# Summing phi(K) of four tiles on GpSimd ahead of the matmuls, with new instruction lists, in a two-layer linear-attention and MLP kernel

## The chip, the cores and the metric

The kernel runs on one core of a Trainium2 chip. The metric is the device time of one execution in microseconds (us); less is better. TensorE (PE) multiplies matrices, VectorE (DVE), ScalarE (ACT) and GpSimd (POOL) work on tiles of 128 partitions, and SyncE (SP) issues transfers. Each engine runs its own list of instructions in order; semaphores order them between engines.

## The reference

Input x has 2048 rows of 512 features in bfloat16. Two layers follow each other with the same weights, each an attention block and an MLP with a residual:

```python
def _A_ref(x, wqkv, wo):                       # 32 heads of 16
    q, k, v = heads_of(x @ wqkv)
    phi = lambda t: jnp.where(t > 0, t + 1, jnp.exp(t)) + 1e-6
    pq, pk = phi(q), phi(k)
    kv = jnp.einsum("bhsd,bhse->bhde", pk, v)
    z = jnp.einsum("bhsd->bhd", pk)            # column sums of phi(K)
    num = jnp.einsum("bhqd,bhde->bhqe", pq, kv)
    den = jnp.einsum("bhqd,bhd->bhq", pq, z)[..., None] + 1e-6
    return rows_of(num / den) @ wo

def _B_ref(x, w1, b1, w2, b2):
    y = _layernorm(x)
    return gelu(y @ w1 + b1) @ w2 + b2

x = x + _A_ref(_layernorm(x), A_wqkv, A_wo)
x = x + _B_ref(_layernorm(x), w1, b1, w2, b2)  # 512 -> 1792 -> 512
```

Both lines come twice. `heads_of` and `rows_of` stand for reshapes.

The change concerns `z`, the sum of phi(K) over all 2048 rows, in the first layer.

## The kernel before

The 2048 rows are four chunks (`c`) of four tiles (`k`) of 128 rows; a tile's number is `st = 4c + k`. The first layer takes the chunks in the order `C0=(3, 0, 1, 2)`, so its first four tiles are 12 to 15. For each tile the kernel normalises the rows, transposes them (four tiles on TensorE, twelve by DMA), multiplies by the K columns of wqkv, forms phi(K), and adds phi(K) against the normalised rows into four PSUM banks (`G`). Q is made by chunk. The products of the first layer are then turned into one matrix per head block (`KV`, `M`), and the MLP follows.

Names of operations, as the lists have them (`0` is the layer, then the chunk or tile):

- `warm`: dummy matmuls on a constant at the start, `N_WARM` of 512 columns and `N_WARM2` of 128 (L699).
- `stats`, `aggr`, `veps`, `pow`, `nmr`, `norm`, `cen`, `ysc`: the steps of a norm (L743, L745, L756, L758, L775, L778 on ScalarE or L783 on VectorE, L724, L768). `pow` is on GpSimd, and so is `nmr`.
- `PTA` and `TA`: the transposes on TensorE (L806) and by DMA on SP's queue (L793).
- `K0_st` (L861), `Q0_c_k` (L892, by tile L879), `G0_st` (L962): groups of four matmuls.
- `exp`, `relu`, `min`, `phi`: the steps of phi (L831, L842, then L844 and L848, or L835 and L837 where `phi` is taken as a maximum straight from PSUM). `phi` of a few tiles is on GpSimd (L848).
- `Z0_c`: the column sums of one chunk's phi(K): 16 matmuls with a single column of ones as the moving operand, phi(K) as the stationary one, four for each of four output columns (L943). `zs0_c` adds the result to `zs` on VectorE (L949, L952).
- `ZH`: the same sums taken from a running total. `za` adds a tile's phi(K) into the float32 tile `zacc` (L915, on GpSimd if not named otherwise), `zhi` and `zlo` split the total into two bfloat16 parts (L921, L924), `ZH` sums these with 8 matmuls (L931, L932), and `zsh` copies the result to `zs` (L935).
- `D0` (L1086), `ln`, `rec` (L1088, L1090), `pr` (L1094): the denominators of chunks 0 and 1 and the products with them, `pr` partly on GpSimd.
- `KV` (L1017), `M` (L1040), `WO` (L1110): into the output projection. `W10`, `W20` (L1142, L1181): the MLP.
- `w1_0`, `w1_1`, `w2_0`, `w2_1`, `wv`, `wo`: the transfers of the weights that the first layer needs late, issued from GpSimd's list (L683). Each waits until the transposes of all sixteen tiles are there. `w1_0` and `w1_1` hold two of w1's four row blocks each, so the first MLP matmul group reads both.

Which chunks go through `za` and `ZH` is set by `ZC`, a pair with one number for each layer: the first `ZC[L]` chunks, in the order in which they come:

```python
n = c if L else C0.index(c)
if n < cf["ZC"][L]:
    ...
    if n < cf["ZC"][L] - 1:
        return
    ...
    return
...
```

The first cut holds the `za`, and the second `zhi`, `zlo`, `ZH` and `zsh`; the last is `Z`.

Before, `ZC` is `(0, 3)`: the first layer sums all chunks by `Z`, the second sums three chunks by `za` and `ZH` and the last by `Z`.

The order of every engine's instructions is written out by hand in `CONF["ORDER"]`, one list for each engine. A small planner runs once at build time over these lists, with costs of its own; it gives each tile its buffer and PSUM bank and from that sets the semaphore waits, but it does not reorder. In the first layer K and Q share four PSUM banks and phi(K) has eight buffers.

Of the kernel before, what the change touches and what calls it, by code (L numbers as in the profile page):

```python
# [282 lines left out]
def assign_waits(graph, order, sems, dma_sems):  # L283
# [10 lines left out]
    while len(done) < total:  # L294
        moved = False
        for e in ENGINES:
# [43 lines left out]
    N_WARM2=9, N_IDLE=[8, 1], XQ='sp', WKQ='sp act', WK1=1,  # L340
    LAND={'x0': 3220, 'x1': 4450, 'wk1': 5200, 'wk0': 6080, 'x2': 6750, 'wq': 8250, 'xc0': 9520, 'xc1': 10800, 'xc2': 12050},
    C0=(3, 0, 1, 2), N_WARM=7, ZC=(0, 3), LQ='sp', N_HALF=1, N_K=4, N_Q=3, P_Z0=6.15, N_PB=1, N_PT=8, P_DEN=-50.43,
# [201 lines left out]
def build_kernel(nc, A_x, A_wqkv, A_wo, B_x, B_w1, B_b1, B_w2, B_b2, out, conf=None, report=False):  # L544
# [5 lines left out]
    with ExitStack() as es:  # L550
# [86 lines left out]

        C0 = cf["C0"]
        HC = C0[0]
# [62 lines left out]
        def idle(name, sizes, after=(), writes=()):  # L702
            return G.op("pe", lambda e: run_idle(e, sizes), sum(sizes) / 1.2, writes=["warm", *writes], tiles=[wu], prio=-300, name=name,
                        n=len(sizes), after=after)
        idle("warm", [D] * cf["N_WARM"] + [P] * cf["N_WARM2"])

# [671 lines left out]
```

## Time and profile before

| | |
|---|---|
| time, median of 3 runs | 325.28 us (325.04 to 326.11) |
| the profiled execution | 324.83 us, of which 323.1 us are the span that the profile shows |
| TensorE busy | 319.6 us, 99% of the span, 1725 matmuls |
| VectorE, ScalarE, GpSimd busy | 215.8, 194.8 and 136.4 us |
| granted TensorE clock | 1.00 |
| first MLP matmul of the first layer | 60.6 us after the span's start |

A line of the timeline gives start, length, engine, line of the kernel, operation, output and inputs, shapes and how many instructions the line stands for; times are in us from the span's start. Instructions of one engine overlap by some tenths in it, so the time that one costs is read from start to start. A table of windows gives busy time by engine for a stretch, then the granted clock, the DMA engines' share and the GB/s that they moved.

### The profile page before, as it was taken

The numbers are of one execution on the slowest core, as the hardware profiler recorded it, in microseconds if no ns is written. First come the engines' busy times: TensorE is split into PE (matmuls) and PEld (weight loads), VectorE is DVE, ScalarE is ACT, GpSimd is POOL, SyncE is SP. The second block draws the span as 40 slices with busy tenths as digits, with TensorE's granted clock in tenths as the row PEclk, the third lists the DMA queues.
The fourth block names the chain that finished last, engine by engine and source line by source line (L and its number), as shares of the span: only waits on it lengthen the run. The fifth ranks groups of instructions, "written<-read, shape, count | busy, mean of one in ns | idle before, by whom it ended". The sixth has DMA issues, their size and how long they took to land.

```text
span 323.1 us, 4792 instructions
## 1 busy us (share of the span) xinstructions
PE 319.6 (99%) x1725; PEld 159.0 (49%) x1725; DVE 215.8 (67%) x506; ACT 194.8 (60%) x334; POOL 136.4 (42%) x224
## 2 busy tenths in 40 slices
PE   8999999999999999999999999999999999999996
PEld 4444445675444444444444444458644444444443
DVE  5998769999985660314659999999898664000232
ACT  6999798873136139488974657879913734576000
POOL 4564376638703359000367645874902934000000
DMA  7534576213320105310003200121242242000004
GB/s 244 178 68 83 148 234 224 49 35 64 67 49 16 35 16 98 67 32 3 0 0 68 49 16 2 25 57 36 50 80 53 49 67 65 16 0 2 32 24 156
DMA packets 48116, 20.65 MB, mean 64 GB/s; under 512 B 43164, under 2 KB 46620, under 8 KB 48092
## 3 DMA queue, kind: packets, MB, share of 16 engines
q1 hardware_dynamic: 46620, 15.32, 20.7%
q0 software_dynamic: 1056, 4.72, 4.6%
q10 hardware_dynamic: 416, 0.30, 0.3%
q8 instruction: 14, 0.23, 0.3%
q14 instruction: 10, 0.08, 0.1%
HBM read 8.00 MB, written 2.10 MB: 31 GB/s over the span
## 4 chain that ended last, share of the span: by engine, by line
PE 92%; DVE 6%; POOL 1%; ACT 0%; issue 0%
PE ps L1142 30%; PE ps L1181 29%; PE ps L861 8%; PE ps L1110 7%; PE ps L962 4%; PE ps L879 3%; PE ps L892 3%; PE ps L994 2%; PE ps L699 1%; PE ps L1168 1%; DVE gtb L1007 1%; DVE rd L1065 1%; PE ps L943 1%; DVE xsb L1115 1%; DVE gacc L1004 1%; PE ps L1086 1%
## 5 line engine op out<-in xcount | busy, mean ns | idle before, releaser
L1148 ACT ACTIVATE gT<-ps,b1c 128x512 bf16<-128x512 f32 (+1 forms) x140 | 77.3, 601 | 64.3 <-PE ps L1142 63.4
L1142 PE MATMUL ps<-t,w 128*128 128x512 bf16 (+1 forms) x560 | 101.2, 336 | 0.0
L1181 PE MATMUL ps<-w,gT 128*128 128x512 bf16 x434 | 98.4, 379 | 0.0
L1142 PEld LDWEIGHTS ps<-t,w 128*128 128x128 bf16 x560 | 54.6, 98 | 43.7 <-ACT t L816 0.3
L1181 PEld LDWEIGHTS ps<-w,gT 128*128 128x128 bf16 x434 | 42.4, 98 | 50.0
L758 POOL TENSOR_TENSOR rstd<-veps,neghalf 128x1 f32<-128x1 f32 x64 | 39.8, 633 | 5.2 <-DVE veps L756 3.0
L1191 DVE TENSOR_TENSOR pkb<-ps,xsb 128x512 bf16<-128x512 f32 x15 | 10.2, 685 | 41.4 <-PE ps L1181 41.4
L831 ACT ACTIVATE eb<-ps 128x512 bf16<-128x512 f32 x56 | 32.4, 598 | 9.0 <-PE ps L879 3.7
L743 DVE BATCH_NORM_STATS2 stats<-xsb 128x6 f32<-128x512 f32 x48 | 32.1, 677 | 0.3
L861 PE MATMUL ps<-wqkv,t 128*128 128x512 bf16 x128 | 31.8, 379 | 0.1
L1110 PE MATMUL ps<-gtb,t 128*128 128x512 bf16 x128 | 31.2, 379 | 0.1
L842 ACT ACTIVATE rb<-ps 128x512 bf16<-128x512 f32 x38 | 22.5, 601 | 10.5 <-PE ps L861 7.2
L748 POOL TENSOR_SCALAR veps<-mv 128x1 f32<-128x1 f32 x32 | 9.1, 283 | 42.8 <-DVE mv L745 40.8
L756 POOL TENSOR_SCALAR veps<-mv 128x1 f32<-128x1 f32 x28 | 7.5, 270 | 44.4 <-DVE mv L745 42.9
L778 ACT ACTIVATE yb<-xsb,nmr,rstd 128x512 bf16<-128x512 f32 x21 | 16.7, 811 | 11.4 <-POOL nmr L775 11.4
L783 DVE TENSOR_SCALAR yb<-xsb,mv,rstd 128x512 bf16<-128x512 f32 x27 | 14.9, 559 | 11.9 <-POOL rstd L758 11.8
L1187 DVE TENSOR_TENSOR xsb<-ps,xsb 128x512 f32<-128x512 f32 x16 | 10.9, 682 | 16.7 <-PE ps L1181 16.7
L879 PE MATMUL ps<-wqkv,t 128*128 128x512 bf16 x80 | 20.4, 379 | 0.0
L861 PEld LDWEIGHTS ps<-wqkv,t 128*128 128x128 bf16 x128 | 12.2, 97 | 15.2 <-ACT t L816 0.6
L1110 PEld LDWEIGHTS ps<-gtb,t 128*128 128x128 bf16 x128 | 12.4, 98 | 14.7 <-ACT gtb L975 0.3
L844 DVE TENSOR_SCALAR eb<-eb 128x512 bf16<-128x512 bf16 x46 | 14.0, 313 | 7.1 <-ACT eb L831 6.9
L1127 POOL TENSOR_TENSOR xsb<-xsb,b2b 128x512 f32<-128x512 f32 x14 | 17.1, 1219 | 1.0 <-DVE yb L783 0.7
(103 smaller groups left out, 393.5 us busy)
## 6 DMA issues: line engine op xcount, KB each, us to landing
w<-in_B_w_dram POOLq DMA_DIRECT2D x4, 896.0 KB, 7.7
out_dram<-pkb SPq DMA_DIRECT2D x15, 128.0 KB, 2.1
t<-in_A_x_dram SPq DMA_DIRECT2D x3, 512.0 KB, 7.0
t<-yb SPq DMA_TRANSPOSE x58, 2.5
wqkv<-in_A_wqkv_dram SPq DMA_DIRECT2D x1, 512.0 KB, 5.4
wqkv<-in_A_wqkv_dram POOLq DMA_DIRECT2D x1, 512.0 KB, 8.6
wo<-in_A_wo_dram POOLq DMA_DIRECT2D x1, 512.0 KB, 4.1
t<-t SPq DMA_TRANSPOSE x20, 2.5
```

What stands on the lines that cost most here:

```text
L743: G.op("dve", lambda e: e.bn_stats(stats[:, s.slot, :], src()), 602, reads=src_keys, writes=[k + "s"], tiles=[s, *src_tiles], prio=prio, n ...
L758: G.op("pool", lambda e: e.tensor_tensor(rstd[:, s.slot:s.slot + 1], veps[:, s.slot:s.slot + 1], neghalf[:], op=ALU.pow), 530, reads=[k + ...
L778: G.op("act", lambda e: e.activation(yb[:, y.slot, :], src(), ACT.Identity, bias=nmr[:, s.slot:s.slot + 1], scale=rstd[:, s.slot:s.slot + 1]),
L831: G.op("act", lambda e: e.activation(eb[:, et.slot, :], bank(bt), ACT.Exp, scale=factor()), 569 if by else 483, reads=[src_key, *more], wr ...
L842: G.op("act", lambda e: e.activation(rb[:, rt.slot, :], bank(bt), ACT.Relu, scale=factor()), 569 if by else 478, reads=[src_key, *more], w ...
L861: ins = e.matmul(bank(b), lhsT=yTa(yT)[:, dt, k * P:(k + 1) * P], rhs=wqkv[:, dt, D:2 * D], start=(dt == 0), stop=(dt == DT - 1))
L879: ins = e.matmul(bank(b), lhsT=yTa(yT)[:, dt, k * P:(k + 1) * P], rhs=wqkv[:, dt, 0:D], start=(dt == 0), stop=(dt == DT - 1))
L1110: ins = e.matmul(bank(wb), lhsT=yTa(pq)[:, kt, k * P:(k + 1) * P], rhs=gtb[:, kt, :], start=(kt == 0), stop=(kt == DT - 1))
L1127: G.op("pool" if on_pool else "dve", lambda e: e.tensor_tensor(xsb[:, st, :], xsb[:, st, :], b2b[:], op=ALU.add), 1120 if on_pool else 600 ...
L1142: ins = e.matmul(bank(b, n), lhsT=w1[:, dt, ft * P:(ft + 1) * P], rhs=yTa(yT)[:, dt, k0 * P:k1 * P], start=(dt == 0), stop=(dt == DT - 1))
L1148: G.op("act", lambda e, ft=ft, b=b, k0=k0, k1=k1, n=n: e.activation(gT[:, g.slot, ft * 512 + k0 * P:ft * 512 + k1 * P], bank(b, n), ACT.Ge ...
L1181: ins = e.matmul(bank(b), lhsT=gT[:, g.slot, ft * 512 + k * P:ft * 512 + (k + 1) * P], rhs=w2[:, ft, :], start=(ft == 0), stop=(ft == FT - 1))
```

## The change

In the first layer the first chunk's phi(K) (tiles 12 to 15) is summed by `za` on GpSimd and `ZH` on TensorE in place of `Z0_3` on TensorE. The dummies at the start become 5 of 512 columns and 17 of 128, from 7 and 9. The lists of all engines are written anew up to the first layer's MLP: from `K0_14` on TensorE's, from tile 13's phi on VectorE's, and to the products `pr0_1` on GpSimd's; behind that they are as before. The functions are unchanged. The diff, with the lists cut:

```diff
-    N_WARM2=9, N_IDLE=[8, 1], ...
+    N_WARM2=17, N_IDLE=[8, 1], ...
-    C0=(3, 0, 1, 2), N_WARM=7, ZC=(0, 3), ...
+    C0=(3, 0, 1, 2), N_WARM=5, ZC=(1, 3), ...
         "pe":
-            "... G0_12_0 K0_14 K0_15 Q0_3_3 G0_13_0 Q0_3_1 K0_0 G0_14_0 K0_1 G0_15_0 G0_0_0 Z0_3 K0_3 Q0_0_3 K0_2
-             Q0_0_0 Q0_0_2 G0_1_0 K0_8 K0_5 G0_2_0 K0_4 Z0_0 G0_3_0 K0_10 K0_6 Q0_0_1 K0_11 K0_7 G0_4_0 K0_9 Q0_1_0
-             Z0_1 Q0_1_2 Z0_2 G0_5_0 Q0_1_3 D0_0_3 Q0_1_1 G0_6_0 ..."
+            "... G0_12_0 K0_14 Q0_3_1 K0_15 Q0_3_3 G0_13_0 K0_0 G0_14_0 K0_1 G0_15_0 K0_3 G0_0_0 K0_2 Q0_0_2 Q0_0_0
+             ZH0 G0_1_0 Q0_0_3 K0_5 G0_2_0 Z0_0 G0_3_0 K0_8 K0_11 K0_4 Q0_0_1 K0_6 K0_10 Q0_1_0 K0_7 Q0_1_1 K0_9
+             G0_4_0 G0_5_0 Z0_1 Z0_2 Q0_1_2 G0_6_0 D0_0_3 Q0_1_3 ..."
         "dve":
-            "... aggrA0_1 phik0_13 yscA0_13 statsA0_8 normA0_1 mink0_14 statsA0_2 phik0_14 aggrA0_2 minq0_3_0 yscA0_14
-             statsA0_5 aggrA0_8 mink0_15 normA0_2 phik0_15 mink0_0 phiq0_3_0 phik0_0 minq0_3_1 statsA0_10 ... zs0_3 ..."
+            "... aggrA0_1 statsA0_10 yscA0_13 minq0_3_0 phik0_13 normA0_1 statsA0_2 statsA0_5 aggrA0_2 mink0_14
+             yscA0_14 phik0_14 aggrA0_5 mink0_15 normA0_2 phiq0_3_0 phik0_15 statsA0_7 statsA0_8 mink0_0 aggrA0_10
+             phik0_0 statsA0_11 minq0_3_2 aggrA0_7 phiq0_3_2 aggrA0_8 mink0_1 zhi0 phik0_1 mink0_3 zlo0 aggrA0_11
+             statsA0_4 phik0_3 zsh0 ..."
         "pool":
-            "... powA0_0 vepsA0_3 vepsA0_1 powA0_1 powA0_3 nmrA0_3 vepsA0_2 powA0_2 vepsA0_8 powA0_8 nmrA0_8 vepsA0_5
-             powA0_5 ... phik0_6 w1_0 wv phiq0_1_2 wo w2_1 w1_1 phiq0_1_1 pr0_0_2 pr0_1_0 pr0_1_1 w2_0 pr0_1_2 pr0_1_3 ..."
+            "... powA0_0 vepsA0_1 vepsA0_3 powA0_1 powA0_3 nmrA0_3 za0_13 vepsA0_2 powA0_2 vepsA0_5 powA0_5 nmrA0_5
+             za0_14 za0_15 vepsA0_10 ... phik0_6 phiq0_1_1 phiq0_1_2 wv wo w1_1 w2_0 w2_1 pr0_1_0 pr0_0_2 pr0_1_1 w1_0
+             pr0_1_2 pr0_1_3 ..."
         "sp":
-            "... xc2 TA0_0 TA0_1 TA0_3 TA0_2 TA0_8 TA0_5 TA0_4 TA0_10 TA0_6 b1 TA0_11 TA0_7 TA0_9 Tb1 b2 ..."
+            "... xc2 b1 TA0_0 TA0_1 TA0_3 TA0_2 TA0_5 TA0_10 TA0_8 TA0_11 TA0_4 TA0_6 TA0_7 TA0_9 Tb1 b2 ..."
```

ScalarE's list has the same instructions in another order up to `expq0_2_2`.

More of the change, by code (lines that the diff above doesn't have):

```diff
@@ L339 @@
 CONF = dict(
-    N_WARM2=9, N_IDLE=[8, 1], XQ='sp', WKQ='sp act', WK1=1,
+    N_WARM2=17, N_IDLE=[8, 1], XQ='sp', WKQ='sp act', WK1=1,
     LAND={'x0': 3220, 'x1': 4450, 'wk1': 5200, 'wk0': 6080, 'x2': 6750, 'wq': 8250, 'xc0': 9520, 'xc1': 10800, 'xc2': 12050},
-    C0=(3, 0, 1, 2), N_WARM=7, ZC=(0, 3), LQ='sp', N_HALF=1, N_K=4, N_Q=3, P_Z0=6.15, N_PB=1, N_PT=8, P_DEN=-50.43,
+    C0=(3, 0, 1, 2), N_WARM=5, ZC=(1, 3), LQ='sp', N_HALF=1, N_K=4, N_Q=3, P_Z0=6.15, N_PB=1, N_PT=8, P_DEN=-50.43,
     P_A2=-55.11, P_W1=38.59, P_W2=10.23, P_K=55.79, P_G=131.85, P_Q=170.13, STEP=3.86, A1_Q=12.91, A1_STEP=0.5, N_H=4,
```

118 rows, old and new, of the table ORDER are left out of this document.

## The prediction

> **What bounds the kernel now.** I read the page first, then TensorE's waits, then the chain of waits in order of time, then the timeline of each engine from 9 to 62 us, which is where the new lists differ from the old.
>
> ```profile
> span 323.1 us, 4792 instructions
> PE 319.6 (99%) x1725; PEld 159.0 (49%) x1725; DVE 215.8 (67%) x506; ACT 194.8 (60%) x334; POOL 136.4 (42%) x224
> ```
> ```profile
> PE ps L699 <- PEq L1363: 0.8, 1, 0.8
> ```
> TensorE is busy 99% of the span, and its only wait of any length is the 0.8 us before its first dummy. So the time is the sum of TensorE's list plus whatever stalls a list gives it, and this list has next to none. Two things follow. Work taken off TensorE is worth its own length and no more. And a new stall costs its full length, because no later gap takes it up.
>
> The profiled execution took 324.83 us; the median of the runs is 325.28, 0.45 above. I sum against 324.83 and add the 0.45 at the end.
>
> **Dummies.** Before: 7x512 + 9x128 = 4736 columns; after: 5x512 + 17x128 = 4736.
>
> ```profile
> 0.83 4.08 PE ps L699 x16
> ```
> 16 dummies took 4.08 us for those columns, so they run by columns, not by number, and the same columns end at the same time. I take 0, with 0.1 either way for six more instructions. The list behind them is unchanged up to K0_14, so the start of TensorE's unbroken run does not move.
>
> **The column sums on TensorE.** Z0_3 (16 matmuls of one column) goes, ZH0 (8) comes. The second layer already runs both forms, ZH1 and Z1_3; from TensorE's timeline:
>
> ```profile
> 190.28 0.17 PE L931 MATMUL ps<-onesm,dz 128*128 128x1 bf16 x1
> ...
> 190.48 1.02 PE L994 MATMUL ps<-pkb,yb 128*128 128x512 bf16 x4
> ...
> 193.06 0.54 PE L943 MATMUL ps<-onesm,pkb 128*128 128x1 bf16 x16
> 193.47 1.89 PE L994 MATMUL ps<-pkb,yb 128*128 128x512 bf16 x8
> ```
> Start to start, ZH1 took 190.48 - 190.28 = 0.20 us and Z1_3 0.41. The change takes **0.20 us** off TensorE. That is all it can gain, 0.06%; about 0.3% (1.0 us) is what a measurement of this kernel can tell from no change.
>
> **The three sums on GpSimd, and VectorE beside them.** za0_13 to za0_15 stand between the small steps of the norms. Layer two's sums show the price (GpSimd's and VectorE's timeline):
>
> ```profile
> 180.44 2.63 POOL L915 TENSOR_TENSOR zacc<-zacc,pkb 128x512 f32<-128x512 f32 x2 [1.90 <-DVE pkb L848]
> ```
> ```profile
> 182.53 0.89 DVE L844 TENSOR_SCALAR eb<-eb 128x512 bf16<-128x512 bf16 x2
> ...
> 187.99 0.41 DVE L921 TENSOR_SCALAR dz<-zacc 128x512 bf16<-128x512 f32 x1
> ...
> 188.53 0.68 DVE L924 TENSOR_TENSOR eb<-zacc,dz 128x512 bf16<-128x512 f32 x1
> ```
> A sum is about 1.3 us, and two minima that came in during the second one took 0.89 us and finished 0.35 after it; the row at 13.79 below is the same instruction undisturbed, 0.28 long and 0.20 from start to start. So a sum holds up a fast VectorE instruction until it is through. In the Trainium skill, SBUF — State Buffer, section Who interferes with whom, VectorE's instructions with a two-port mode or two SBUF inputs and GpSimd's lock each other out for a whole instruction, whoever starts first. By that rule, which these rows bear out, three sums could hold VectorE for up to 3 x 1.3 = 3.9 us if it met each at its start. zhi0, zlo0 and zsh0 add about 1 us more to VectorE, but behind phi(K) of tiles 1 and 3, ahead of nothing that is due.
>
> Where it matters is phi(K) of tiles 14 and 0, on VectorE, GpSimd and TensorE:
>
> ```profile
> 12.21 0.17 DVE L745 BATCH_NORM_AGGREGATE mv<-stats 128x2 f32<-128x6 f32 x1
> 12.30 0.39 DVE L848 TENSOR_TENSOR pkb<-eb,rb 128x512 bf16<-128x512 bf16 x1
> 12.61 0.35 DVE L768 TENSOR_SCALAR yb<-yb,rstd 128x512 bf16<-128x512 bf16 x1
> 12.87 0.69 DVE L743 BATCH_NORM_STATS2 stats<-t 128x6 f32<-128x512 bf16 x1
> 13.48 0.39 DVE L783 TENSOR_SCALAR yb<-t,mv,rstd 128x512 bf16<-128x512 bf16 x1
> 13.79 0.28 DVE L844 TENSOR_SCALAR eb<-eb 128x512 bf16<-128x512 bf16 x1
> 13.99 0.68 DVE L743 BATCH_NORM_STATS2 stats<-t 128x6 f32<-128x512 bf16 x1
> 14.60 0.40 DVE L848 TENSOR_TENSOR pkb<-eb,rb 128x512 bf16<-128x512 bf16 x1
> ...
> 17.52 0.68 DVE L837 SCALAR_TENSOR_TENSOR pkb<-ps,eb 128x512 bf16<-128x512 f32 x1
> ```
> ```profile
> 14.03 0.27 POOL L775 TENSOR_SCALAR nmr<-mv,rstd 128x1 f32<-128x1 f32 x1
> ```
> ```profile
> 16.14 1.03 PE L962 MATMUL ps<-pkb,yb 128*128 128x512 bf16 x4
> 17.01 1.03 PE L861 MATMUL ps<-wqkv,t 128*128 128x512 bf16 x4
> 17.87 1.89 PE L962 MATMUL ps<-pkb,yb 128*128 128x512 bf16 x8
> ```
> VectorE runs without a gap here, so starts give prices: aggr 0.09, phi 0.31, ysc 0.26, stats 0.61, norm 0.31, min 0.20; a TensorE group of four is 0.86. phik0_14 (14.60 to 15.00) was 1.14 us ahead of its reader G0_14 (16.14). The new list puts ten instructions between 12.30 and phik0_14: three stats 1.83, two ysc 0.52, two min 0.40, one phi 0.31, one norm 0.31, one aggr 0.09, together 3.46. It starts at 15.76 and ends at 16.16, while G0_14 keeps its place on TensorE (the same groups ahead of it). The cover is gone: a stall of about 0.05 without GpSimd. za0_13 follows nmrA0_3, which ended at 14.30 and whose first step now stands behind tile 1's, so it runs from about 14.5 to 15.8, over mink0_14, due at 15.30: about 0.3 more. Then phik0_0: behind phik0_14, from 16.06 on, stand aggr, min, norm, two phi, two stats, min, aggr, 3.04 with phik0_14 itself; phik0_0 adds 0.68 and ends at 19.8, near 20.0 if normA0_2 waits for its pow behind za0_13. G0_0, one group later than its 18.73 and 0.35 late, is due at 19.95. I take 0.05 there (0 to 0.4, as za0_14 and za0_15 hold a minimum or not). **+0.40 us** in all; bounds 0 and 0.8.
>
> **Other moves up to there.** b1's small transfer goes to the head of SP's transposes; it waits for a GpSimd memset, and the first transpose waits for its norm anyway. TA0_8 moves behind TA0_5 and TA0_10, and K0_8 moves back with it. ScalarE has the same instructions. I cost these at nothing; without their cover each costs a few tenths, inside the bounds above.
>
> **The weights on GpSimd's queue.** The change's few words don't name this part. Before, w1_0 and wv were issued right behind phik0_6, wo, w2_1, w1_1 behind phiq0_1_2, w2_0 last. Now phiq0_1_1 and phiq0_1_2 stand ahead of all six, the order is wv, wo, w1_1, w2_0, w2_1, and w1_0, which the first MLP matmul reads, comes last, behind three products pr0.
>
> ```profile
> 34.64 0.94 POOL L683 DMA_DIRECT2D w<-in_B_w_dram  x1
> ...
> 40.70 1.15 POOL L848 TENSOR_TENSOR t<-eb,rb 128x512 bf16<-128x512 bf16 x1 [4.31 <-DVE eb L844]
> ...
> 42.57 1.69 POOL L683 DMA_DIRECT2D w<-in_B_w_dram  x2
> ...
> 49.65 2.40 POOL L1094 TENSOR_TENSOR t<-t,lr 128x512 bf16<-128x512 bf16 x2 [1.20 <-ACT lr L1090]
> 51.99 0.98 POOL L683 DMA_DIRECT2D w<-in_B_w_dram  x1
> ```
> ```profile
> 37.28 1.02 PE L892 MATMUL ps<-t,wqkv 128*128 128x512 bf16 x4
> ...
> 60.61 1.58 PE L1142 MATMUL ps<-t,w 128*128 128x256 bf16 x13
> ```
> phiq0_1_2's matmuls (Q0_1_2, 37.28) stand 1.9 us later in the new list, plus the 0.40: they end near 40.6, and exp, relu and minimum bring GpSimd's sum to about 41.8 to 43.0. wv goes out then, at 43.0 against some 35.6 (34.64 + 0.94). The whole of the weights now has to pass between there and the MLP, due at 60.61 - 0.20 + 0.40 = 60.8:
>
> ```profile
> w<-in_B_w_dram POOLq DMA_DIRECT2D x4, 896.0 KB, 7.7
> ...
> wqkv<-in_A_wqkv_dram POOLq DMA_DIRECT2D x1, 512.0 KB, 8.6
> wo<-in_A_wo_dram POOLq DMA_DIRECT2D x1, 512.0 KB, 4.1
> ```
> ```profile
> 43.00:52.50 9.50, 9.50 (x58) 4.81 (x56) 8.45 (x18) 8.98 (x18) 6.36 (x7) 1.00 0.75 250
> 48.00:50.00 2.00, 2.00 (x22) 1.38 (x21) 1.63 (x5) 2.00 (x4) 0.80 (x2) 1.00 1.00 391
> 53.50:57.10 3.60, 3.60 (x18) 1.63 (x17) 3.53 (x8) 2.08 (x4) 2.83 (x4) 1.00 0.86 254
> 43.50:50.00 6.50, 6.50 (x43) 3.44 (x42) 5.45 (x11) 6.24 (x12) 3.43 (x5) 1.00 0.90 297
> ```
> ```profile
> DMA to landing us min/median/max: 5.8/5.8/5.8
> ```
> (The last column is GB/s; the landing is w2_0's.) Four of 896 KB and two of 512 KB are 4.72 million bytes. w2_0, alone, was issued at 51.99, moved from 53.5 to 57.1 and landed at 57.8: data from 1.5 us after the issue begins (1.3 for wv, whose issue is shorter), and 0.7 from the last data to the landing. So wv's data would start at 44.3. wo, w2_1 and w1_1 went at 250 GB/s over all, at 297 without their ends, at 391 in their best 2 us. At 391 the six take 12.1 us and land at 57.1; at 250, 18.9 us and 63.9. Behind each other they save some of the slow starts; nearest is the 250, and I take 270: 17.5 us, data to 61.8, landing at 62.5. (w1_0's own issue, near 52 behind the three products, is no bound: 52 + 5.8 is 57.8.) **The stall ahead of the first MLP matmul is 62.5 - 60.8 = 1.7 us**; bounds 0 and 3.1. wv, at the head of the queue, is in by 47, 1.5 us ahead of KV0_0, which stands 12 us before the MLP in TensorE's list; wo follows 2 us later and is due 2 us later.
>
> A second price of the same move: the transposes of layer norm's first tiles, which the MLP reads too, would now share the DMA engines with weights. I add nothing for it, as both delays run at the same time.
>
> **Sum.** 324.83 - 0.20 + 0.40 + 1.7 = 326.7; on the median, **327.2 us**.
>
> **Rivals.**
> - *The weights are in time.* The point that decides: 4.72 MB between 44.3 and 60.1 (0.7 ahead of 60.8) is 299 GB/s; the row of 297 all but reaches it. Then only the stall on phi(K) is left: 325.28 - 0.20 + 0.40 = 325.5. In the Trainium skill, DMA: Bandwidth & Descriptors, section Where 436 GB/s comes from, about 358 GB/s is the bound from HBM; by it, as an estimate, the six take 13.2 us and this rival is what happens. In this trace the best 2 us passed that rate, and no stretch of 6 us came near it. Chance 0.24.
> - *Not slower: the sums slip between VectorE's slow instructions,* as in layer two, where stats and PSUM reads ran beside them undelayed, and the weights are in time. Decided by whether mink0_14 meets za0_13. Then 325.28 - 0.20 = 325.1. Chance 0.12.
> - *VectorE becomes the bound.* Each sum meets a fast instruction near its start and costs 0.8 to 1.1, and phik0_14 and phik0_0 are late by up to 1.5: 325.28 - 0.20 + 1.5 = 326.6 with the weights in time. For it: VectorE has no gap from 9 to 28 us. Against it: half of its time there is stats, which nothing held. Chance 0.06.
> - That the change doesn't do what it says can be left out: the built order shows 8 matmuls, three sums and the moved transfers.
>
> **Numbers.** The forecast, late weights, has 0.58; its own range is 325.9 to 328.6 (stalls of 0.4 to 3.1). Low end 325.0: the gain alone with 0.1 for the dummies. High end 329.0: 325.28 - 0.20 + 0.8 + 3.1. Slower by over 0.3%: 0.58 less the tenth of it with a stall under 0.8, plus the third rival, 0.56. Within: 0.40. Faster by over 0.3% has no term that reaches 1 us: 0.04, for what I haven't seen.
>
> **What would show it.** In the profile after: TensorE's list has a gap just ahead of its first L1142 row and its weight load there waits for a DMA of w; w1_0 is issued near 52 and lands after 60.8; L962 stands still for some tenths at 16 to 20 us with VectorE's L848 or L837 named. Wrong if the first L1142 starts by 61.0, if the weights pass at 300 GB/s or more, or if TensorE has a gap past 65 us.

## The result and the profile after

| | before | after |
|---|---|---|
| median | 325.51 us (6 runs, 325.04 to 326.11) | 327.28 us (6 runs, 326.31 to 327.51) |
| ratio | | 1.0051, 95% interval 1.0037 to 1.0065 |
| the profiled execution, its span | 324.83, 323.1 us | 327.49, 325.7 us |
| first MLP matmul of the first layer | 60.61 us | 63.29 us |

Slower by 0.5%. The page of the kernel after:

```profile
span 325.7 us, 4797 instructions
PE 320.1 (98%) x1723; PEld 159.0 (49%) x1723; DVE 218.6 (67%) x508; ACT 195.4 (60%) x334; POOL 140.1 (43%) x227
```

TensorE is as busy as before; the span is longer by stalls. TensorE's waits, after (us in total, times, longest), and TensorE's timeline around the start of the MLP:

```profile
PE ps L1142 <- issue: 1.0, 1, 1.0
PE ps L699 <- PEq L1363: 0.8, 1, 0.8
PE ps L861 <- DMA wqkv<-in_A_wqkv_dram: 0.8, 1, 0.8
PE ps L861 <- DMA t<-yb: 0.3, 1, 0.3
```
```profile
61.00 0.39 PE L806 MATMUL ps<-idp,yb 128*128 128x128 bf16 x4
61.23 1.04 PE L1110 MATMUL ps<-gtb,t 128*128 128x512 bf16 x4
63.29 2.89 PE L1142 MATMUL ps<-t,w 128*128 128x256 bf16 x25 [1.02 <-issue]
```

There is the gap that was forecast ahead of the first MLP matmul: the last matmul of L1110 starts at 61.89, a matmul of 512 columns takes 0.216 from start to start, and L1142 starts at 63.29; that is 1.19 us. (Gaps below are reckoned in this way.) "issue" means that the profile found no releaser. The forecast's releaser was w1_0. Its issue, with the time to its landing:

```profile
L683 POOL DMA_DIRECT2D w<-in_B_w_dram x1: 772/772/772, 53.6 to 53.6; - x1
...
DMA to landing us min/median/max: 7.6/7.6/7.6
```

53.61 + 7.62 is 61.23: 0.9 us before L1142 could have started (61.89 + 0.22), and 2 us before it did. The other operand is the transposed norm, and its last part for this group is TB0_1. Its issue after, and the same before:

```profile
L793 SPq DMA_TRANSPOSE t<-yb x1: 1217/1217/1217, 59.6 to 59.6; - x1
...
DMA to landing us min/median/max: 3.7/3.7/3.7
```
```profile
L793 SPq DMA_TRANSPOSE t<-yb x1: 1207/1207/1207, 58.1 to 58.1; - x1
...
DMA to landing us min/median/max: 2.5/2.5/2.5
```

Issued at 59.55, it landed at 63.20, 0.09 before L1142 started. It took 3.65 us; before, 2.46. Before, it landed at 60.51, 0.10 ahead of the first MLP matmul, so there was no slack there either. What moved in the DMA queues while its packets ran, after (60.5 to 62.8 us) and then before (58.9 to 60.2 us; packets, MB, share of the engines):

```profile
q1 hardware_dynamic: 544, 0.13, 61.9%
q8 instruction: 1, 0.02, 3.0%
q0 software_dynamic: 4, 0.00, 0.1%
```
```profile
q1 hardware_dynamic: 544, 0.13, 49.7%
```

q1 is the transpose. The weights (q0) had all but ended. New is one packet of 16 KB in the queue for instructions, at 60.67, 1.09 us long; before, that fetch came at 57.26, ahead of the transpose. Such a packet comes 13 or 14 times in an execution, on average with every 250 or so of TensorE's matmuls and weight loads.

The front of the kernel: VectorE, GpSimd and TensorE after.

```profile
15.73 0.17 DVE L745 BATCH_NORM_AGGREGATE mv<-stats 128x2 f32<-128x6 f32 x1
15.81 0.52 DVE L844 TENSOR_SCALAR eb<-eb 128x512 bf16<-128x512 bf16 x1
16.25 0.34 DVE L768 TENSOR_SCALAR yb<-yb,rstd 128x512 bf16<-128x512 bf16 x1
16.52 0.41 DVE L848 TENSOR_TENSOR pkb<-eb,rb 128x512 bf16<-128x512 bf16 x1
```
```profile
15.03 1.16 POOL L915 TENSOR_TENSOR zacc<-pkb 128x512 f32<-128x512 bf16 x1
```
```profile
15.89 1.03 PE L861 MATMUL ps<-wqkv,t 128*128 128x512 bf16 x4
16.98 1.04 PE L962 MATMUL ps<-pkb,yb 128*128 128x512 bf16 x4
...
19.59 1.03 PE L861 MATMUL ps<-wqkv,t 128*128 128x512 bf16 x4
20.65 1.04 PE L962 MATMUL ps<-pkb,yb 128*128 128x512 bf16 x4
22.01 1.04 PE L861 MATMUL ps<-wqkv,t 128*128 128x512 bf16 x4 [0.33 <-DMA t<-yb]
```

mink0_14 (15.81) takes 0.52 instead of 0.28 and ends only when za0_13 (15.03 + 1.16) is through; phik0_14 follows at 16.52. A group of four is 0.86, so G0_14 (16.98) is 0.23 late, G0_0 (20.65) 0.20, and K0_2 (22.01) 0.49, where TA0_2 took 4.14 us, with a fetch 1.8 us behind its issue. A gap of 0.14 follows, ahead of a K group's matmul at 30.53. Between 16 and 34 us the gaps of 0.05 and more make 1.06 us, where before had 0.08.

### The profile page after: what moved, and what is told of

The parts are those of the page before. It is cut to its first block, busy times and chain, and to the rows that moved or that the text cites. A ratio compares the mean times of both kernels' runs of the same rounds, so it can differ in the third digit from the quotient of the medians.

```text
span 325.7 us, 4797 instructions
## 1 busy us (share of the span) xinstructions
PE 320.1 (98%) x1723; PEld 159.0 (49%) x1723; DVE 218.6 (67%) x508; ACT 195.4 (60%) x334; POOL 140.1 (43%) x227
## 4 chain that ended last, share of the span: by engine, by line
PE 86%; DVE 8%; DMA 3%; POOL 1%; issue 1%; ACT 1%; SPq 0%
PE ps L1142 30%; PE ps L1181 29%; PE ps L1110 7%; PE ps L861 7%; PE ps L892 3%; PE ps L962 3%; PE ps L994 2%; PE ps L879 2%; DVE stats L743 2%; DMA t<-in_A_x_dram 2%; DMA t<-yb 1%; PE ps L1168 1%; POOL rstd L758 1%; DVE gtb L1007 1%; DVE rd L1065 1%
## 5 line engine op out<-in xcount | busy, mean ns | idle before, releaser
L1142 PE MATMUL ps<-t,w 128*128 128x512 bf16 (+1 forms) x560 | 101.2, 336 | 1.0 <-issue 1.0
L1142 PEld LDWEIGHTS ps<-t,w 128*128 128x128 bf16 x560 | 54.7, 98 | 44.7 <-issue 1.5
L1110 PE MATMUL ps<-gtb,t 128*128 128x512 bf16 x128 | 31.2, 379 | 0.1
L748 POOL TENSOR_SCALAR veps<-mv 128x1 f32<-128x1 f32 x32 | 8.9, 277 | 43.1 <-DVE mv L745 41.0
L1110 PEld LDWEIGHTS ps<-gtb,t 128*128 128x128 bf16 x128 | 12.3, 98 | 14.7 <-ACT gtb L975 0.3
```

The source lines that it names most:

```text
L1110: ins = e.matmul(bank(wb), lhsT=yTa(pq)[:, kt, k * P:(k + 1) * P], rhs=gtb[:, kt, :], start=(kt == 0), stop=(kt == DT - 1))
L1142: ins = e.matmul(bank(b, n), lhsT=w1[:, dt, ft * P:(ft + 1) * P], rhs=yTa(yT)[:, dt, k0 * P:k1 * P], start=(dt == 0), stop=(dt == DT - 1))
```

## The experiments

Theories. **W1**, the prediction's: w1_0 is late. **W2**: the tail of the weights slows TB0_1. **F**: the 16 KB instruction fetch slows it. **V**: the sums on GpSimd hold VectorE. **L**: the order of the new lists alone makes the front's gaps. Ratios below are to the kernel before, run beside each.

**weights_back.** GpSimd's list of the changed kernel from phik0_6 on as it was before:

```diff
-phik0_6 phiq0_1_1 phiq0_1_2 wv wo w1_1 w2_0 w2_1 pr0_1_0 pr0_0_2 pr0_1_1 w1_0 pr0_1_2 pr0_1_3
+phik0_6 w1_0 wv phiq0_1_2 wo w2_1 w1_1 phiq0_1_1 pr0_0_2 pr0_1_0 pr0_1_1 w2_0 pr0_1_2 pr0_1_3
```

> The changed kernel with one part undone: GpSimd's list from phik0_6 to pr0_1_3 as it was before (w1_0 and wv first, w2_0 last). Three theories of the 1.2 us gap ahead of the first MLP matmul. W1, the prediction's: w1_0 itself is late. Its trace row in the changed kernel says no (landed 61.2, the matmul was due at 62.3), but under it the gap goes and the time falls by 1.2, to 326.1. W2: the tail of the late weights delays the transpose TB0_1, which landed 3.65 us after its issue instead of 2.46. Then TB0_1 lands in about 2.5 us, the gap goes, 326.1 as well. F: an instruction fetch of 16 KB (at 60.67 in the changed kernel, 57.26 before), which falls among that transpose's packets, delays it. Then the fetch stays where it is, TB0_1 still takes 3.5 or more, the gap stays at about 1.0 and the time at 327.2.

Measured: 328.81 us, 1.0099 (1.0083 to 1.0114): slower than the changed kernel, which no theory said. TB0_1 took 2.43 us and the gap just ahead of the MLP is gone, but gaps of 1.51 us in all came in earlier, at KV and M, and 0.75 more at the last L1110 group and within the MLP. TensorE's wait there, and VectorE and GpSimd ahead of it:

```profile
PE ps L1016 <- DVE gtb L977: 0.6, 1, 0.6
```
```profile
46.84 1.24 DVE L834 TENSOR_SCALAR eb<-eb 128x512 bf16<-128x512 bf16 x1
```
```profile
46.64 1.29 POOL L847 TENSOR_TENSOR t<-eb,rb 128x512 bf16<-128x512 bf16 x1
```

phiq0_1_1, behind three transfers again, met a minimum of VectorE at its start and held it for its whole length, 0.28 made into 1.24; the copies of G (gtb) began at 49.32 instead of 48.22. So in the new order this phi(Q) gains by going before the weights. For W2 and F the run is of no use: all was 1.5 us later, TB0_1 was issued at 61.18, behind the weights' landing and behind the fetch (60.35).

**fetch_early.** The changed kernel with more and narrower dummies:

```diff
-N_WARM2=17, ... N_WARM=5, ...
+N_WARM2=33, ... N_WARM=1, ...
```

> The changed kernel with N_WARM=1 and N_WARM2=33 in place of 5 and 17: the same 4736 dummy columns, 12 matmuls more. Every 16 KB fetch of the instruction queue comes about 256 TensorE instructions (matmuls and weight loads) after the last, so 12 more matmuls, 24 instructions, should bring each about 2.5 us forward: from 19.7 to about 17, and from 60.7 to about 58, which is before the packets of TB0_1 (60.5 to 62.75). F (the fetch delays the transposes): TB0_1 lands in about 2.5 us, the gap ahead of the first MLP matmul shrinks from 1.2 to 0.2 or less, the one of 0.49 ahead of K0_2 may go too; time 325.8 to 326.3. W2 (the weights' tail delays TB0_1): nothing moves, gap 1.0 to 1.2, 327.2.

Measured: 328.12 us, 1.0070 (1.0056 to 1.0083). The fetch came at 57.80 and TB0_1 took 2.62; the gap fell from 1.19 to 0.16, while the weights were still on their way (w1_0 landed at 62.11). So W2 is worth 0.16 at most. The time did not fall. In the profiled execution the tenth fetch had moved as well, onto a transpose of the second layer (and a gap of 0.97 ahead of K0_12 is the landing of wk1, at 6.79). TensorE's timeline at the second MLP, and the landings of TB1_2 and TB1_3:

```profile
224.90 1.36 PE L1142 MATMUL ps<-t,w 128*128 128x256 bf16 x11 [1.61 <-ACT gT L1148]
```
```profile
L793 SPq DMA_TRANSPOSE t<-yb x2: 1188/1188/1189, 219.1 to 220.5; - x2
...
DMA to landing us min/median/max: 2.5/3.4/4.3
```

The second transpose, issued at 220.54 with a fetch at 222.51, landed at 224.81, and the matmuls went on at 224.90, after a gap of 1.77. The wait is put down to a gelu, the last releaser that the profile found; the landing, 0.09 ahead as in the changed kernel, speaks for the transpose. K0_2's gap went too, and one of the same 0.49 stood at K0_5 in its place.

**dummies_only.** The kernel before with the new dummies:

```diff
-N_WARM2=9, ... N_WARM=7, ...
+N_WARM2=17, ... N_WARM=5, ...
```

> The kernel before with the narrower dummies alone (5 of 512 columns and 17 of 128 for 7 and 9). The prediction: nothing, 325.5 (within 0.1). Rival S: the gap of 0.95 us ahead of K0_12 in the changed kernel (0.22 before), where wk1 and wk0 landed 1.15 and 0.57 later, comes with the dummies (more instructions to be fetched at the start, beside those transfers): then it is here too, and the time is 326.2. If the landings are only uneven from run to run, the gap has nothing to do with either.

Measured: 325.43 us, 1.0001 (0.9988 to 1.0014): nothing, as predicted. The profiled execution took 326.91, 1.5 above its median: it has a gap of 1.42 in the front, where TA0_1 took 4.45 us with a fetch 2.0 us behind its issue.

**no_sums.** The changed kernel with its lists, less the sums:

```diff
-ZC=(1, 3), ...  K0_3 G0_0_0 K0_2 Q0_0_2 Q0_0_0 ZH0 ...  za0_13 ... za0_14 za0_15 ...  zhi0 ... zlo0 ... zsh0 ...
+ZC=(0, 3), ...  K0_3 G0_0_0 Z0_3 K0_2 Q0_0_2 Q0_0_0 ...  zs0_3 ...
```

> The changed kernel without the sums: ZC=(0, 3), Z0_3 behind G0_0_0 in place of ZH0, zs0_3 where zhi0 stood; all else of the new lists is kept. V (the GpSimd sum holds VectorE's fast minimum and with it phi(K), as the prediction says): mink0_14 takes 0.3 instead of 0.52, the gaps ahead of G0_14 (0.23) and G0_0 (0.20) go, TensorE gets 0.2 back; time 327.28 - 0.43 + 0.2 = 327.1. L (the order of VectorE's list alone makes those gaps, with phik0_14 ten instructions later): the gaps stay at about 0.4 in all, 327.5. Under both, the gap ahead of the MLP is as in the changed kernel, unless the 8 more matmuls move the fetch.

Measured: 327.10 us, 1.0042 (1.0028 to 1.0056), on the figure of V; but V and L differ by less than the interval, and VectorE's timeline has to tell:

```profile
15.73 0.17 DVE L744 BATCH_NORM_AGGREGATE mv<-stats 128x2 f32<-128x6 f32 x1
15.81 0.26 DVE L843 TENSOR_SCALAR eb<-eb 128x512 bf16<-128x512 bf16 x1
15.99 0.34 DVE L767 TENSOR_SCALAR yb<-yb,rstd 128x512 bf16<-128x512 bf16 x1
16.25 0.42 DVE L847 TENSOR_TENSOR pkb<-eb,rb 128x512 bf16<-128x512 bf16 x1
```

With the same start to the hundredth (15.73), phik0_14 comes 0.27 sooner, and G0_14 has no gap. TensorE was 0.37 later there, but phik0_14 was over at 16.67, in time also for the 16.75 at which G0_14 was due in the changed kernel: V, for this gap. The one at G0_0 is gone as well, behind a gap of 0.72 ahead of K0_1, where TA0_1 was hit by a fetch (3.93 us). The MLP's gap is 0.93 with TB0_1 at 3.40, so it has nothing to do with the sums.

**fetch_late** and **before_late.** The changed kernel, and the kernel before, with fewer and wider dummies:

```diff
-N_WARM2=17, ... N_WARM=5, ...      (changed kernel)
+N_WARM2=1, ... N_WARM=9, ...
-N_WARM2=9, ... N_WARM=7, ...       (kernel before)
+N_WARM2=1, ... N_WARM=9, ...
```

> The changed kernel with its dummies as 9 of 512 columns and 1 of 128: the same 4736 columns, 12 matmuls fewer. In the six traces so far, every DMA transpose with a 16 KB instruction fetch between 0.1 and 2.3 us after its issue took 2.6 to 4.5 us, and the others 2.4 to 2.6. The third fetch comes at 710 to 738 TensorE instructions (matmuls and weight loads) whatever the kernel, so 24 instructions fewer put it about 2.6 us later, at 61.5 to 63.3. F (the fetch delays the transposes): past 61.9 it misses TB0_1 (issued 59.55), which then lands in 2.5 us; the gap of 1.2 ahead of the MLP falls to 0.2 and the one of 0.49 ahead of K0_2 (fetch from 19.7 to about 22) goes too: 325.8. W2 (the late weights delay TB0_1): gap and time stay, 327.2.

> The converse: the kernel before, where no transpose that something waits for is hit, with dummies of 9 x 512 and 1 x 128 columns: the same columns, 6 matmuls fewer, and nothing else. Its third fetch should move from 57.3 to between 58.5 and 59.5, into the 2.3 us behind TB0_1's issue at 58.1. F: TB0_1 takes 3.5 instead of 2.46, TensorE gets a gap of about 1.0 ahead of the first MLP matmul, and the time is 326.5. If fetches do not matter, 325.5. No weights are in flight there after 57.8, so W2 has nothing to give a gap.

Measured: 326.77 us, 1.0037 (1.0024 to 1.0049), and 325.40 us, 0.9995 (0.9987 to 1.0004). The fetches did not go where I meant them to: the third came at 694 and 699 of TensorE's instructions, 0.36 us behind the issue of TB0_1 in the one and 0.96 ahead of it in the other. By F's own rule the first is a light hit: TB0_1 took 3.05, the gap was 0.59. The profile names the transpose this time:

```profile
PE ps L1142 <- DMA t<-yb: 0.4, 1, 0.4
```

The second is a miss: 2.46 us, no gap. The rule held, the steering did not; the converse on the kernel before has therefore not been shown at this place. At another the old lists have such gaps too: in before_late 0.91 ahead of Q0_0_3, which started 0.13 behind the landing of TA0_2 (a fetch 1.9 us behind its issue, 4.91 us).

**sums_alone** and **sums_alone_2.** The sums put into the old lists, with the old dummies and with nine more:

```diff
-N_WARM2=9, ... N_WARM=7, ZC=(0, 3), ...
+N_WARM2=9, ... N_WARM=7, ZC=(1, 3), ...      (sums_alone)
+N_WARM2=21, ... N_WARM=4, ZC=(1, 3), ...     (sums_alone_2)
```

In both, ZH0 and Z0_0 stand behind K0_10 on TensorE's list.

> The sums without the new lists: the kernel before with ZC=(1, 3). za0_13, za0_14 and za0_15 stand behind nmrA0_3, nmrA0_8 and nmrA0_10 on GpSimd's list, zhi0 and zlo0 behind mink0_8 on VectorE's, ZH0 and Z0_0 behind K0_10 on TensorE's; the rest keeps its order, and the weights go out as before. V (sums hold VectorE): phik0_14 is over before za0_13 starts, so no gap at G0_14; zhi0 and zlo0 put 1.0 on VectorE late, with at most some tenths at ZH0. F: 8 matmuls fewer put the third fetch 1.7 us later, to about 59.0, onto TB0_1: gap about 1.0, 325.5 - 0.2 + 1.0 = 326.3. Without F: 325.3.

> The kernel of sums_alone with 4 dummies of 512 columns and 21 of 128 (again 4736 columns), 9 matmuls more, which give back the 8 that the sums save. F: the third fetch is again near 57.1, ahead of TB0_1's issue at about 58.0; no gap ahead of the MLP, 325.3, about 1.0 less than sums_alone, and the fastest of all so far by 0.2. Without F: 325.3 as well, but then the same as sums_alone.

Measured: 332.61 us, 1.0212 (1.0187 to 1.0238), and 333.04 us, 1.0214 (1.0195 to 1.0233). Both expectations missed by 6 to 8 us. TensorE's waits in sums_alone:

```profile
PE ps L930 <- DVE pkb L836: 1.4, 1, 1.4
PE ps L891 <- DMA t<-yb: 1.3, 1, 1.3
...
PE ps L942 <- DVE zs L934: 0.7, 1, 0.7
```

L930 is ZH0. zlo0 was over at 31.76, yet ZH0 started at 34.23, when a phi had read its K from PSUM (33.49 + 0.68). Z0_0 behind it waited for zsh0, and the next K for zs0_0, which read PSUM as well: 1.56, 0.81 and 0.39 us, in both kernels. The two results now stand in PSUM one behind the other in a place where every bank is wanted. TB0_1 took 2.46 in both, so they say nothing on F. Within the first MLP 1.8 us more of gaps follow in both, which I have not traced. The two runs say that at this place the sums cost more in the old order than in the new; other places were not tried.

**tb1_on_pe** and **sums_later.** The changed kernel with tile 1's transpose on TensorE; and with the first sum later besides:

```diff
-TB0_1 by DMA ...  WO0_4_0 WO0_6_0 PTB0_0 ...  tcB0_0 ...
+TB0_1 on pe ...   WO0_4_0 PTB0_1 WO0_6_0 PTB0_0 ...  tcB0_1 tcB0_0 ...
```
```diff
-nmrA0_3 za0_13 vepsA0_2 ... nmrA0_5 za0_14 za0_15
+nmrA0_3 vepsA0_2 ... nmrA0_5 za0_13 za0_14 za0_15   (sums_later)
```

> The changed kernel with the transpose of layer norm's tile 1 on TensorE (PTB0_1 ahead of WO0_6_0, its copy on ScalarE) in place of the DMA transpose TB0_1; nothing else moves, and w1_0 goes out where it did. If TB0_1 alone is what the first MLP matmul waits for (so far its gap was TB0_1's time less 2.46 in every trace: 1.19, 0.93, 0.59, 0.16), the gap goes, whatever the fetch does, and TensorE has 0.22 more: 327.28 - 1.19 + 0.22 = 326.3. If w1_0 (the prediction) or the tail of the weights holds the MLP beside it, a gap stays ahead of the first L1142 with a DMA of w named, and the time is about 327.2.

> The kernel of tb1_on_pe with za0_13 behind nmrA0_5, so that the three sums run back to back from about 18.6 to 22.0 instead of the first from 15.0 to 16.2. V (za0_13 holds mink0_14): mink0_14 takes 0.28 instead of 0.52, the gap of 0.23 ahead of G0_14 goes; that of 0.20 ahead of G0_0 stays or goes too, zhi0 waits some tenths, and TA0_10 and TA0_8 come 1.1 later, with up to 0.4 ahead of K0_8. Time 326.3 - 0.2 to + 0.2. L (the order of VectorE's list makes the gap): it stays at 0.23.

Measured for tb1_on_pe: 326.53 us, 1.0041 (1.0026 to 1.0056). The MLP starts without a gap:

```profile
61.12 1.03 PE L1110 MATMUL ps<-gtb,t 128*128 128x512 bf16 x4
61.98 2.71 PE L1142 MATMUL ps<-t,w 128*128 128x256 bf16 x23
```

w1_0 had landed at 60.43, issued where it was in the changed kernel. That settles the wait: TB0_1 and nothing else. In time it is 0.38 less than the changed kernel run beside it (326.91, after_again below), with 0.22 more on TensorE; the intervals overlap, so it is the trace that shows it. The front's gaps are still there, 1.06 us of the 1.3 by which it is slower than the kernel before. For sums_later: 327.38 us, 1.0073 (1.0057 to 1.0089). mink0_14 took 0.26, phik0_14 came 0.52 behind aggr again and G0_14 had no gap, as V says; but the gap at G0_0 stayed (0.19): that one is the order's, as L says. K0_2 had 0.71, with a fetch 2.36 behind the issue of TA0_2, ZH0 came in with 0.53, and K0_5 with 0.47. A minimum at 21.07 took 1.22 beside the last sum: the sums only moved what they hold.

**weights_moved.** The kernel before with the weights behind both phi(Q):

```diff
-phik0_6 w1_0 wv phiq0_1_2 wo w2_1 w1_1 phiq0_1_1 pr0_0_2 pr0_1_0 pr0_1_1 w2_0 pr0_1_2 pr0_1_3
+phik0_6 phiq0_1_2 phiq0_1_1 wv wo w1_1 w2_0 w2_1 pr0_0_2 pr0_1_0 pr0_1_1 w1_0 pr0_1_2 pr0_1_3
```

> The disputed step of the prediction by itself: the kernel before, with GpSimd's list from phik0_6 on as phiq0_1_2 phiq0_1_1 wv wo w1_1 w2_0 w2_1 pr0_0_2 pr0_1_0 pr0_1_1 w1_0 pr0_1_2 pr0_1_3, that is the weights behind both phi(Q) and w1_0 last; all else as before. The prediction (270 GB/s): w1_0 lands about 1.7 us after it is due, time 325.5 + 1.7 = 327.2. At the 328 GB/s of the changed kernel's trace the weights are in at about 60, w1_0 in time, and what is left is W2: their tail beside TB0_1 (issued 58.1), at most 0.2 by the trace of fetch_early. Then 325.5 to 325.7, as long as no fetch falls behind TB0_1's issue.

Measured: 330.44 us, 1.0180 (1.0150 to 1.0210), missed by all. GpSimd's timeline, TensorE's wait, and two windows behind it (the last three columns are the granted clock, the DMA share and GB/s):

```profile
46.91 1.18 POOL L847 TENSOR_TENSOR t<-eb,rb 128x512 bf16<-128x512 bf16 x1 [4.19 <-ACT rb L841]
48.03 0.98 POOL L682 DMA_DIRECT2D wqkv<-in_A_wqkv_dram  x1
```
```profile
PE ps L1016 <- DMA wqkv<-in_A_wqkv_dram: 3.3, 1, 3.3
```
```profile
52.90:55.60 2.70, 2.70 (x19) 2.06 (x20) 0.00 (x0) 1.35 (x3) 2.00 (x3) 0.51 1.02 353
56.00:60.00 4.00, 4.00 (x21) 1.76 (x18) 3.81 (x9) 3.22 (x6) 1.62 (x3) 1.00 1.02 361
```

In the old order phiq0_1_1 is over at 48.0 only (in the changed kernel at 43.1), so wv, first of the weights, lands at 52.78 and KV0_0 waits for it: 3.5 us, and then 1.3 of half clock. The late weight that costs is wv, and the changed kernel escapes it by 1.0 us: there wv landed at 48.95 and KV0_0 started at 49.96.

**after_again.** The changed kernel once more.

> The changed kernel once more, to see what is the kernel's and what is one execution's. Steady, by V: the gaps of 0.23 and 0.20 ahead of G0_14 and G0_0. If the third fetch is bound to a count of TensorE's instructions (710 to 738 in most traces, 694 in one), it falls between 59.7 and 61.9 again, TB0_1 takes 3.0 or more, and the gap ahead of the MLP is 0.6 to 1.2; time 327.2. The gap ahead of K0_12 follows the landing of wk1, which was 5.2 to 6.8 in the traces so far without a pattern by kernel: 0.2 to 1.0.

Measured: 326.91 us, 1.0057 (1.0037 to 1.0076). The fetch came at 59.61, 0.10 behind the issue of TB0_1, which took 2.76; gap 0.30. K0_2 had no gap this time (TA0_2 took 3.30), and K0_5 has one of 0.48, from 26.01 on:

```profile
26.49 0.39 PE L861 MATMUL ps<-wqkv,t 128*128 128x512 bf16 x1 [0.32 <-ACT eb L831]
```

**All traces together on TB0_1** (us, from the packets and landings of each; difference: fetch less issue):

| kernel | issue | fetch | difference | took | gap at the MLP |
|---|---|---|---|---|---|
| before | 58.06 | 57.26 | -0.80 | 2.46 | 0 |
| dummies_only | 60.13 | 59.20 | -0.93 | 2.46 | 0 |
| before_late | 59.35 | 58.39 | -0.96 | 2.46 | 0 |
| weights_moved | 63.73 | 63.34 | -0.39 | 2.45 | 0 |
| weights_back | 61.18 | 60.35 | -0.83 | 2.43 | 0 |
| fetch_early | 60.01 | 57.80 | -2.21 | 2.62 | 0.16 |
| after_again | 59.51 | 59.61 | +0.10 | 2.76 | 0.30 |
| fetch_late | 59.41 | 59.77 | +0.36 | 3.05 | 0.59 |
| no_sums | 59.83 | 60.60 | +0.77 | 3.40 | 0.93 |
| after | 59.55 | 60.67 | +1.12 | 3.65 | 1.19 |

The two sums_alone kernels (differences of -1.2 and -1.1) took 2.46 as well. The gap is the time of TB0_1 less 2.46, to 0.01, in every row with a gap, and from a difference of 0.10 on the time grows with it. In after and no_sums, the two longest, the weights' last packets ended before the transpose's first, which came 1.2 us behind its issue: they had nothing left to slow it with.

## Why the prediction was right in the sum and wrong in its main step

- **What bounds the kernel; the dummies at 0; TensorE's 0.20.** Right: TensorE is 98% busy, dummies_only measured 1.0001, and ZH0 took 0.21 (24.61 to 24.82).
- **The sums, 0.40.** Right in size (0.23 at G0_14 and 0.20 at G0_0), and in cause for the first. The sum of 1.16 us held mink0_14; without it (no_sums) or with it later (sums_later) the 0.23 goes. This bears out the rule of the Trainium skill, SBUF — State Buffer, section Who interferes with whom; weights_back has the plainest row of it, 1.24 us for a minimum. The 0.20 at G0_0 stays in sums_later, so it is the new order's, for which I had 0.05.
- **"Other moves up to there" at nothing.** Mis-sized: some 0.6 us, K0_2 or K0_5 with 0.5 to 0.6 and up to 0.15 behind them. In the six profiles of the changed lists with the sums in their place (after, after_again, weights_back, fetch_early, fetch_late, tb1_on_pe) the gaps from 16 to 34 us add up to 1.02 to 1.08 us, of which I had 0.40. They stand at K0_2 when a fetch hits TA0_2, and else at K0_5; so the fetch alone is not their cause. At K0_5 the traces lead to the sums, by a way that I had not priced: GpSimd's own list. nmr of tile 8 and ScalarE's norm behind it, in after_again and then in no_sums:

```profile
24.10 0.51 POOL L775 TENSOR_SCALAR nmr<-mv,rstd 128x1 f32<-128x1 f32 x1
24.65 0.81 ACT L778 ACTIVATE yb<-t,nmr,rstd 128x512 bf16<-128x512 bf16 x1 [0.35 <-POOL nmr L775]
```
```profile
22.77 0.52 POOL L774 TENSOR_SCALAR nmr<-mv,rstd 128x1 f32<-128x1 f32 x1
24.98 0.80 ACT L777 ACTIVATE yb<-t,nmr,rstd 128x512 bf16<-128x512 bf16 x1
```

  In after_again GpSimd had worked without a pause since za0_14 (18.53), the norm waited 0.35 for nmr, the two exps behind it ended at 26.43, and K0_5, which by the profile waits for the second, started at 26.49. In no_sums nmr was over 1.3 us earlier and the norm did not wait. TensorE was 1.1 us later there, so this is read from the traces; no run shows it by itself.
- **The weights, 1.7 us: the step that failed.** It was the rate, 270 GB/s. The windows of the changed kernel (last column GB/s):

```profile
46.00:60.40 14.40, 14.40 (x81) 7.01 (x79) 13.62 (x28) 11.86 (x23) 11.02 (x14) 1.00 0.96 328
53.00:60.40 7.40, 7.40 (x36) 3.38 (x35) 7.29 (x14) 5.45 (x12) 5.39 (x8) 1.00 0.97 354
```

  wv went out 1.4 us later than I had reckoned (44.45 instead of 43.0), the MLP was due 1.3 later as well (62.1 instead of 60.8), and w1_0 landed at 61.23, in time. A full queue ran at 354 GB/s in its second half; I had taken my rate from windows that held the starts and ends of the old kernel's transfers. About 358, which the Trainium skill states in DMA: Bandwidth & Descriptors, section Where 436 GB/s comes from, was the better guide. My own test for it, 300 GB/s or more, came out against me.
- **"A second price of the same move", at nothing.** There was the stall: TB0_1, one of the transposes that I named and dropped. The weights delay it by 0.16 at most; the rest, 0.30 to 1.19 us in four profiles of the new lists, goes with an instruction fetch. Neither side of the sum had a fetch in it.
- **The sum.** In the profiled execution, span against span: 0.73 ahead of K0_12 (below), 0.98 in the front, 1.19 at the MLP, -0.20, and -0.1 elsewhere: the 2.6 us. That 327.2 came out is luck: 1.7 us that did not exist were replaced by 0.6 in the front and by the fetch. Of the rivals, "the weights are in time" was the true premise, with a wrong price (325.5). (The chance of a time over 0.3% longer adds up to 0.58 from its terms; I wrote 0.56.)
- **Noise of one profile.** The 0.73 ahead of K0_12 is wk1 landing at 6.36 instead of 5.21. Over all fourteen profiles, of both kinds of lists, it landed between 5.0 and 6.8; this is the execution's, not the change's.

No kernel here beats the one before; dummies_only and before_late equal it.

## What to carry to other kernels

When the operand that was feared late is in time, look at the landing of the other one: of a matmul that waits for "issue", or for an engine that has long been done, compare its start with the landings of all DMAs that it reads. Give a DMA transpose that something waits for an extra 1 to 2.5 us of lead (4.91 instead of 2.46 us was the longest here), or do the first one on TensorE: one profile shows only where that execution's instruction fetches happened to fall. And a moved transfer has more than one reader: price the earliest (wv here), with the time that its new place in the queue takes in this order of work.

## What the runs showed of the hardware

- **Instruction fetches and DMA transposes.** The fourteen profiles hold 1090 DMA transposes (b1's small one left out). 880 of them had no fetch of 16 KB or 8 KB between 0.9 us before and 2.3 us after their issue: 877 took 2.40 to 2.56 us, one took 2.62, and two, with a 16 KB fetch 2.31 and 2.36 behind the issue, 4.34 and 4.36. All 73 with a 16 KB fetch 0.1 to 2.1 us behind their issue took longer, 2.66 to 4.91 us, and so did 21 of the 24 with one from 0.5 ahead of it to 0.1 behind (TB0_1 of weights_moved is one of the three that did not). With an 8 KB fetch alone, all 21 that had it 1.0 to 2.1 us behind took 2.75 to 3.87. This is a coincidence in time; no run could take the fetch away. The third 16 KB fetch came at 691 to 738 of TensorE's instructions (its semaphore waits counted in). Changing the count of dummies moved it, but not by a predictable amount. Why it fell 0.4 to 1.2 us ahead of TB0_1 in all six profiles of the old lists, and behind it in four of the six of the new, is not settled.
- **Half clock after a stall.** In weights_moved TensorE waited 3.33 us and then ran at 0.51 for some 2.7 us (window above). In the Trainium skill, TensorE: Matmul & The Clock Gate, section Why this matters for your kernels, idle gaps of about 3 us bring the clock back to half; this agrees. sums_alone and sums_alone_2 had the same three shorter gaps (1.56, 0.81 and 0.39 within 3.5 us) and differ: the first, which had one of 1.49 ten us earlier too, then ran at half clock, the second did not. Their windows behind the gaps:

```profile
36.30:39.60 3.30, 3.30 (x9) 1.15 (x8) 2.16 (x6) 1.26 (x3) 0.35 (x1) 0.51 0.20 41
```
```profile
36.50:39.80 3.30, 3.30 (x16) 1.52 (x17) 2.33 (x6) 2.00 (x5) 0.79 (x1) 1.00 0.20 41
```
